# Loading and casting the wide pieces of w_in in parts by contraction block

## Chip, cores, metric

One core of a Trainium2 chip; the three later calls of runs ran on three different chips, and each ratio compares runs of one call. The metric is the device time of one execution in microseconds (us), the median of several. The profile's span is some 2 us shorter than that time.

## The reference

```python
# q, k, v: (8, 8, 576, 64) float32; moe_w_in: (512, 2048); moe_w_out: (2048, 512)
q_s = softmax(q, axis=-1); k_s = softmax(k, axis=2)
kv  = einsum('bhsd,bhse->bhde', k_s, v)
a   = einsum('bhsd,bhde->bhse', q_s, kv)          # attention without a score matrix
x   = a.transpose(0, 2, 1, 3).reshape(4608, 512)
out = (gelu_exact(x @ moe_w_in) @ moe_w_out)      # float32
```

## The kernel before

Nine token blocks of 512 pass through a hidden phase (16 row tiles of x @ w_in with GELU; four matmuls, "dm", make a tile) and an output phase. The attention of later batches is spread into these phases. During the first hidden phase, the weights and the inputs of batches 1 to 3 are still arriving. All loads go through one queue, in program order.

```python
    def h_phase(c, ins, group=1, pre={}):
        ...
        for t0 in [0] + list(range(group, NDF)):
            ...
            for dm in range(NDM):
                ...
                for ps, t in zip(pss, ts):
                    nc.tensor.matmul(
                        ps, wi_bf[:, dm, t * 128:(t + 1) * 128], xT[:, dm, :],
                        start=(dm == 0), stop=(dm == NDM - 1),
                    )
            for ps, t in zip(pss, ts):
                nc.scalar.activation(out=g[:, t, :], in_=ps, func=AF.Gelu)
                for f in ins.get(t, []):
                    f()
    ...
    wi = [load_wi(i) for i in range(5)]
    wo = [load_wo(i) for i in range(3)]
    load_main(1, "q", q, 2)
    load_pair(1, "k", k, 2)
    wo.append(load_wo(3, 2))
    load_pair(1, "v", v, 4)
    load(2)
    nc.vector.memset(zeros, 0.0)
    setup_tiles()
    warm(30)                         # matmuls on zeros while the first inputs arrive
    ... # attention of batch 0
    h_phase(0, {
        0: [lambda: cast_wi(2, wi[2], "v")],
        2: [lambda: cast_wi(3, wi[3], "v")],
        4: [lambda: cast_wi(4, wi[4], "v")],
        ...
    }, group=2, ...)
    ... # output phase 0 with the attention of batch 1, hidden phase 1
    load(3)                          # q, k, v of batch 3
    exp_q(2, parts=2)
    exp_k(2)
    exp_q(3)
    exp_k(3)
    table(AF.Gelu)
    y_phase(1, {
        ...
        (1, 15): [lambda: xbar_step(2)],   # DMA transpose of q of batch 2
        (3, 3): [lambda: x_step(2, 0)],    # its first use by PE
        ...
    })
```

The softmax here doesn't subtract the row's maximum and nothing guards it: scores larger than these inputs give would overflow.

## Time and profile before

| | before |
|---|---|
| time, 3 runs at first | 288.45 us median (288.38 to 288.96) |
| span of the profiled run | 286.4 us |
| PE busy | 277.5 us, 97% |

PE (TensorE) is the bound. The prediction reads the rest of the profile, with its lines.

### The profile page before, as it was taken

The numbers are of one execution on the slowest core, as the hardware profiler recorded it, in microseconds if no ns is written. First come the engines' busy times: TensorE is split into PE (matmuls) and PEld (weight loads), VectorE is DVE, ScalarE is ACT, GpSimd is POOL, SyncE is SP. The second block draws the span as 40 slices with busy tenths as digits, with TensorE's granted clock in tenths as the row PEclk, the third lists the DMA queues.
The fourth block names the chain that finished last, engine by engine and source line by source line (L and its number), as shares of the span: only waits on it lengthen the run. The fifth ranks groups of instructions, "written<-read, shape, count | busy, mean of one in ns | idle before, by whom it ended". The sixth has DMA issues, their size and how long they took to land.

```text
span 286.4 us, 3707 instructions
## 1 busy us (share of the span) xinstructions
PE 277.5 (97%) x1464; PEld 132.4 (46%) x1491; DVE 116.3 (41%) x211; ACT 153.6 (54%) x211; POOL 38.6 (13%) x34
## 2 busy tenths in 40 slices
PE   8969999999999999999999999999999999999995
PEld 3524455445445445444544454445444444444443
DVE  7654387217694553344324522362225112110012
ACT  5766684779465824584368526761664165016500
POOL 5830033002020050005000500040002200000000
PEclk9999999999999999999999999999999999999999
DMA  7999999998519939922994289616701600120033
GB/s 231 374 382 387 371 389 304 319 292 218 146 45 251 298 105 243 263 82 76 224 282 116 76 187 276 163 73 159 136 2 58 157 7 0 64 83 2 0 72 74
DMA packets 58384, 50.04 MB, mean 175 GB/s; under 512 B 26496, under 2 KB 48256, under 8 KB 58368
## 3 DMA queue, kind: packets, MB, share of 16 engines
q1 hardware_dynamic: 58208, 49.68, 61.3%
q8 instruction: 11, 0.18, 0.3%
q10 hardware_dynamic: 160, 0.13, 0.1%
q14 instruction: 5, 0.04, 0.0%
HBM read 36.70 MB, written 9.44 MB: 161 GB/s over the span
## 4 chain that ended last, share of the span: by engine, by line
PE 89%; DMA 6%; ACT 2%; issue 1%; DVE 1%; SPq 0%; ACTq 0%
PE ps L340 42%; PE ps L350 40%; DMA w<-in_moe_w_in_dram 4%; DMA f<-in_k_dram 2%; PE ps L309 2%; PE ps L237 2%; PE ps L372 1%; ACT ek L152 1%; PE ps L241 0%; ACT L152 0%; DVE wi_bf L416 0%; PE ps L183 0%; ACT e L152 0%; SPq L105 0%; PE ps L314 0%
## 5 line engine op out<-in xcount | busy, mean ns | idle before, releaser
L345 ACT ACTIVATE g<-ps 128x512 bf16<-128x512 f32 x144 | 85.8, 597 | 104.7 <-PE ps L340 104.7
L340 PE MATMUL ps<-xT,wi_bf 128*128 128x512 bf16 x560 | 131.0, 379 | 2.6 <-DVE wi_bf L416 1.2
L350 PE MATMUL ps<-wo_bf,g 128*128 128x512 bf16 x549 | 123.2, 379 | 0.6
L340 PEld LDWEIGHTS <-wi_bf 128*128 128x128 bf16 x576 | 55.5, 98 | 66.8 <-DVE wi_bf L416 1.7
L350 PEld LDWEIGHTS <-g 128*128 128x128 bf16 x560 | 54.6, 98 | 64.9
L357 DVE COPY y_sb<-ps 128x512 f32<-128x512 f32 x35 | 23.9, 688 | 75.6 <-PE ps L350 72.6
L229 POOL TENSOR_TENSOR e<-e,recq 128x1024 bf16<-128x1024 bf16 (+1 forms) x10 | 27.6, 2760 | 179.6 <-DVE recq L228 141.5
L322 DVE CAST xT<-ps 128x512 bf16<-128x512 f32 x33 | 22.8, 691 | 36.2 <-PE ps L309 27.6
L227 DVE TENSOR_REDUCE qsum<-e 128x16 f32<-128x1024 bf16 (+1 forms) x13 | 21.1, 1622 | 9.0 <-ACT e L152 8.9
L152 ACT ACTIVATE e<-f 128x1024 bf16<-128x1024 f32 (+1 forms) x11 | 15.8, 1442 | 4.4 <-DMA f<-in_q_dram 4.3
L210 DVE CAST v_aug<-f 128x512 bf16<-128x512 f32 x24 | 10.3, 429 | 9.9 <-DMA f<-in_v_dram 9.3
L309 PE MATMUL ps<-qT,kvbd 128*128 128x512 bf16 x32 | 12.2, 381 | 0.8 <-ACT kvbd L196 0.6
L94 ACT ACT_TABLE_LOAD x9 | 11.5, 1283 | 0.9 <-PEq L616 0.7
L152 ACT ACTIVATE ek<-f 128x2048 bf16<-128x2048 f32 x6 | 11.4, 1894 | 0.0
L436 PE MATMUL ps<-kvbd 128*128 128x512 bf16 x35 | 10.0, 452 | 1.2 <-DVE scr L82 1.2
L168 ACT ACTIVATE ek<-f 64x1152 bf16<-64x1152 f32 x8 | 9.3, 1162 | 1.7 <-DMA f<-in_k_dram 1.6
L237 PEld LDWEIGHTS <-ek 128*128 128x128 bf16 x96 | 6.8, 97 | 3.1 <-ACT ek L152 0.6
L237 PE MATMUL ps<-v_aug,ek 128*128 128x129 bf16 x96 | 8.1, 220 | 0.1
L152 ACT ACT_TABLE_LOAD x6 | 7.7, 1283 | 0.1
L427 DVE CAST wo_bf<-w 128x2048 bf16<-128x2048 f32 (+1 forms) x5 | 5.1, 1014 | 5.3 <-DMA w<-in_moe_w_out_dram 5.1
L259 DVE TENSOR_TENSOR kvbd<-ps,rec 64x128 bf16<-64x128 f32 x24 | 6.9, 289 | 0.6
L436 PEld LDWEIGHTS <-kvbd 128*128 128x128 bf16 x35 | 3.8, 114 | 6.4 <-issue 2.8
(46 smaller groups left out, 83.7 us busy)
## 6 DMA issues: line engine op xcount, KB each, us to landing
out_dram<-y_sb SPq DMA_DIRECT2D x32, 256.0 KB, 2.4
f<-in_q_dram SPq DMA_DIRECT2D x6, 1024.0 KB, 8.0
f<-in_k_dram SPq DMA_DIRECT2D x6, 1024.0 KB, 10.9
f<-in_v_dram SPq DMA_DIRECT2D x6, 1024.0 KB, 9.9
w<-in_moe_w_in_dram SPq DMA_DIRECT2D x3, 1024.0 KB, 12.5
w<-in_moe_w_out_dram SPq DMA_DIRECT2D x3, 1024.0 KB, 12.2
f<-in_k_dram SPq DMA_DIRECT2D x4, 576.0 KB, 8.3
f<-in_v_dram SPq DMA_DIRECT2D x8, 288.0 KB, 8.5
```

Source lines behind the costliest of these rows:

```text
L94: nc.scalar.activation(out=scr[:, 1:2], in_=scr[:, 0:1], func=func)
L152: nc.scalar.activation(out=dst[:, i * n:(i + 1) * n], in_=src[:, i * n:(i + 1) * n], func=AF.Exp)
L227: nc.vector.reduce_sum(out=qsum, in_=eq[:, :, hs, :], axis=AX.X)
L229: eng.tensor_tensor(out=eq[:, :, hs, :], in0=eq[:, :, hs, :], in1=recq.unsqueeze(3).to_broadcast([128, J, w, D]), op=ALU.mult,)
L237: nc.tensor.matmul(ps, st[b]["ek"][:, j, hs, :].rearrange("p h d -> p (h d)"), v_aug[b % 2][:, j, hp, 0:PW], start=(j == 0), stop=False,)
L309: nc.tensor.matmul(ps, kvbd[b][:, hp, :], st[b]["qT"][:, :, hp, :], start=True, stop=True)
L322: nc.vector.tensor_copy(out=st[b]["xT"][:, hp, :], in_=ps)
L340: nc.tensor.matmul(ps, wi_bf[:, dm, t * 128:(t + 1) * 128], xT[:, dm, :], start=(dm == 0), stop=(dm == NDM - 1),)
L345: nc.scalar.activation(out=g[:, t, :], in_=ps, func=AF.Gelu)
L350: nc.tensor.matmul(ps, st[c]["g"][:, t, j * 128:(j + 1) * 128], wo_bf[:, t, :], start=(t == 0), stop=(t == NDF - 1),)
L357: nc.vector.tensor_copy(out=y_sb, in_=ps)
L436: nc.tensor.matmul(ps, zeros[:, 0:128], zeros, start=True, stop=True)
```

## The change

The intent: PE should start on the third piece's first contraction block while the last one is still coming. In the diff, `groups={0: 2}` does what `group=2` did; the moved cast keeps its place in VectorE's order.

```diff
-    def h_phase(c, ins, group=1, pre={}):
+    def h_phase(c, ins, groups={}, pre={}):
...
     wi_cols = [256, 256, 512, 512, 512]
+    wi_parts = [1, 1, 4, 2, 2]
     wi_off = [0, 256, 512, 1024, 1536]
 
     def load_wi(i):
+
         w = wst.tile([128, NDM, 512], FP32, tag="w")
         n = wi_cols[i]
-        nc.sync.dma_start(
-            out=w[:, :, 0:n],
-            in_=moe_w_in[:, wi_off[i]:wi_off[i] + n].rearrange("(c p) f -> p c f", p=128),
-        )
+        src = moe_w_in[:, wi_off[i]:wi_off[i] + n].rearrange("(c p) f -> p c f", p=128)
+        d = NDM // wi_parts[i]
+        for c in range(0, NDM, d):
+            nc.sync.dma_start(out=w[:, c:c + d, 0:n], in_=src[:, c:c + d])
         return w
...
-            nc.vector.tensor_copy(out=o, in_=w[:, :, 0:n])
+            d = NDM // wi_parts[i]
+            for c in range(0, NDM, d):
+                nc.vector.tensor_copy(out=o[:, c:c + d], in_=w[:, c:c + d, 0:n])
...
-        4: [lambda: cast_wi(4, wi[4], "v")],
+        6: [lambda: cast_wi(4, wi[4], "v")],
```

More of the change, by code (lines that the diff above doesn't have):

```diff
@@ L331, in h_phase @@
         xT = st[c]["xT"]
-        for t0 in [0] + list(range(group, NDF)):
-            ts = range(t0, t0 + (group if t0 == 0 else 1))
+        t1 = 0
+        while t1 < NDF:
+            t0, t1 = t1, t1 + groups.get(t1, 1)
+            ts = range(t0, t1)
             pss = [psum_h.tile([128, M], FP32, tag="h", name="ps") for t in ts]
@@ L482 @@
         2: [lambda: cast_wi(3, wi[3], "v")],
-        4: [lambda: cast_wi(4, wi[4], "v")],
+        6: [lambda: cast_wi(4, wi[4], "v")],
         9: [lambda: cast_wo(0, wo[0])],
         12: [lambda: cast_wo(1, wo[1])],
-    }, group=2, pre={
+    }, groups={0: 2}, pre={
         1: [lambda: x_step(0, 2)],
@@ L537 @@
         12: [lambda: cast_v_all(2)],
-    }, group=2, pre={
+    }, groups={0: 2}, pre={
         1: [lambda: x_step(1, 3, "s")],
```

## The prediction

> **What bounds the kernel now.** I read the page first, then the chain of waits, then single stretches of the timeline. The page says that the matrix engine is busy for 277.5 of 286.4 us, at the full clock. So only some 9 us can be won by removing waits. The chain that ended last, by engine:
>
> ```profile
> PE 89%; DMA 6%; ACT 2%; issue 1%; DVE 1%; SPq 0%; ACTq 0%
> ```
>
> The 6% of DMA and the 1% of DVE sit in the first 21 us, so I took the same chain in that window:
>
> ```profile
> 1.79 6.37 DMA f<-in_k_dram
> 8.15 0.02 issue
> 8.17 11.47 DMA w<-in_moe_w_in_dram
> 19.64 0.02 issue
> 19.66 1.24 DVE wi_bf L416
> 20.90 0.05 issue
> 20.95 7.30 PE ps L340 x33
> ```
>
> Columns: start, duration, what. The third piece of w_in (1 MiB, columns 512 to 1023, row tiles 4 to 7 of the first hidden phase) lands at 19.64 us, is cast as a whole by VectorE until 20.90, and only then does PE begin tile 4. What PE lost shows in the waits of PE over the whole run (waiter, releaser, total us, times, longest) and in its timeline:
>
> ```profile
> PE ps L340 <- DVE wi_bf L416: 1.2, 1, 1.2
> PE ps L436 <- DVE scr L82: 1.2, 1, 1.2
> ```
> ```profile
> 16.75 2.97 PE L340 MATMUL ps<-xT,wi_bf 128*128 128x512 bf16 x12
> 20.95 10.53 PE L340 MATMUL ps<-xT,wi_bf 128*128 128x512 bf16 x47 [1.23 <-DVE wi_bf L416]
> 31.32 1.03 PE L350 MATMUL ps<-wo_bf,g 128*128 128x512 bf16 x4
> ```
>
> It happened once, and it is the largest single wait that PE has (the other 1.2 is the start). The 1.23 us counts from a modelled end of a matmul. Counted in issue slots: tiles 4 to 15 are 48 matmuls, (31.32 - 20.95) / 48 = 0.216 us each. The last matmul of tile 3 began at 16.75 + 2.97 - 0.38 = 19.34, so the next could have begun at 19.56. It began at 20.95: 1.39 us lost. That is the most the change can win here. Pieces four and five cost PE nothing: no other wait for L416 is listed.
>
> DMA is the other half of the picture. In every half-microsecond from 6.5 to 30 us it moves 346 to 419 GB/s at full share, so 1 MiB takes about 2.7 us (1.049 MB / 0.386) and no byte can come sooner by reordering the issue alone.
>
> **What the Trainium skill says.** "VectorE: DVE Perf Modes", section "The perf-mode tier table", gives 1227 ns for a float32 copy of 2048 elements; the trace has 1227 for L416. Its section "The TRN2 errata" says a fixed cost is paid per instruction, so small ones pay more. The trace agrees: 1227 ns for 2048 and 694 for 1024 elements make 0.52 ns per element plus 161 ns fixed, so my estimate for 512 is 428 ns. "DMA: Bandwidth & Descriptors", section "Bandwidth", advises batches of 1 MiB or more and shows 64 KB far below peak. The trace does not show that loss in a full queue: v's four 288 KB parts complete at 10.39, 11.14, 11.89 and 12.66 us in the completion records, 0.75 us apart or 393 GB/s. "Runtime: NRT & Kernel Launch", section "Instruction fetch mechanics", says that instructions are refilled by DMA in blocks of 16 KiB. The page's instruction queue has 11 packets; the packet records put one of 16,384 bytes at 17.45 us for 1.11 us. It falls into our piece: its first engine completes at 17.64 and its last at 19.64, a spread of 2.00 where the piece before had 0.74. I expect it there again, so the end of the piece stays late.
>
> **The change part by part.**
>
> 1. Loads. Three issues become eight; bytes, row length (2 KB) and order stay. Piece three comes in four 256 KB parts, each one block of the contraction; pieces four and five in halves. Each extra issue costs SyncE about 0.45 us (v's parts), 5 x 0.45 = 2.3 us. SyncE waits from 12.8 to 15.4 us anyway, and the queue has about 7 us of bytes ahead.
>
> 2. Semaphores. In the built program eight of them serve the loads in turn, so an issue waits for the load eight places before. With smaller loads these eight cover fewer bytes. I went through the list: the last w_in half waits for the second narrow w_in piece (15.66 us), when three wide pieces, some 7 us of transfer, are still queued or moving. The first w_out piece goes from 15.42 to about 17.6, its two followers to about 18.3 and 20.1. By then at least 2.5 MiB are ahead. The queue should not run dry, and landings stay.
>
> 3. Casts. 3 x 1227 = 3681 ns become 4 x 428 + 4 x 694 = 4488 ns: 0.81 us more on VectorE, which sits idle 2.32, 1.33 and 1.47 us before the three casts. Off the path. The cast moved from tile 4 to tile 6 keeps its place in VectorE's order, as the ordered listing of both kernels shows.
>
> 4. The wait. The first three parts land by 18.96 at an even rate (19.64 - 0.68) and are cast by 19.4. The last lands at 19.64 and is cast by 19.66 + 0.43 = 20.09; with 0.05 to signal, 20.14. PE starts tile 4 at 19.56 on part one; part four is wanted at 19.56 + 3 x 0.216 = 20.21. No wait is left: 1.39 us earlier. Tile 8 is then wanted at 23.0; its halves land near 20.9 and at 22.19, cast by 21.6 and 22.9. Tile 12 at 26.5; cast by 25.6.
>
> 5. What takes some back. PE next meets transfers at 40 to 46 us. These lines are of the timeline there (POOL, then PE, then DVE):
>
> ```profile
> 42.58 0.66 POOL L174 CAST v_aug<-f 128x576 bf16<-128x576 f32 x1 [3.36 <-DMA f<-in_v_dram]
> 43.33 0.67 POOL L174 CAST v_aug<-f 128x576 bf16<-128x576 f32 x1
> ```
> ```profile
> 41.68 1.06 PE L274 MATMUL ps<-identity,e 128*128 128x128 bf16 x16
> 42.57 1.89 PE L350 MATMUL ps<-wo_bf,g 128*128 128x512 bf16 x8
> 44.30 0.45 PE L183 MATMUL ps<-v_aug,ek 128*128 128x65 bf16 x9
> ```
> ```profile
> 38.70 1.59 DVE L229 TENSOR_TENSOR e<-e,recq 128x1024 bf16<-128x1024 bf16 x1
> 40.44 0.69 DVE L427 CAST wo_bf<-w 128x1024 bf16<-128x1024 f32 x1
> ```
>
> All of these except PE's are held by transfers (q, w_out, v of batch 1), which do not come sooner. PE 1.39 earlier would transpose at 40.29; its second half, at 40.82, wants the DVE product of 40.29: fits. It would resume the output matmuls at 41.18; the cast ends at 41.13: just fits. It would want v at 42.91; the first POOL cast ends at 43.24, about 43.30 with the signal: 0.39 us of new wait. The following v parts, POOL-cast by 44.00 and so on, are wanted later than that. Sum: 1.39 - 0.39 = 1.00 us.
>
> 6. After 50 us PE waits for no transfer in the waits view; exponentials and normalisations follow PE and ScalarE, so the 1.00 us should last to the end. Prediction: 288.45 - 1.0 = 287.45 us.
>
> **Rivals.** First, the gain is given back at 43 us: if v of batch 1 landed 0.5 us later, or a cast of w_out became last, only 0.5 would remain (288.0). For it speaks that PE would arrive within 0.1 us of three other events; against it that the queue was saturated and stays in order. Second, more and smaller loads starve the queue: the eight semaphores then hold fewer bytes, and each hole delays all that follows. A hole of 1 us would bring back 288.4, one of 2 us 289.4. Against it: v's parts at 393 GB/s, and the count of queued bytes in step 2. Third, the whole 1.39 stays (287.05), if v happened to land sooner; a saturated queue speaks against it. Fourth, the parts do not help because PE waits for the whole region: then nothing changes (288.45). The changed program has separate waits of PE for each block of tile 4, which speaks against it.
>
> **Range and chances.** The steps give 286.9 to 288.0 and three runs before spread over 0.6 us, so I take 286.9 to 288.2. Two per cent is 5.8 us, over four times the removable wait, so faster by that is next to impossible; slower by that would need several holes in the queue. Faster 0.01, same 0.98, slower 0.01.
>
> **What would show it.** Right: PE runs from tile 3 into tile 4 near 19.56 us, with no wait for the wide w_in casts; four casts of about 428 ns, the last starting near 19.66; PE reaches the output phase near 29.9; a new wait of about 0.4 us for the POOL cast of v near 43; afterwards everything 1.0 us earlier. Wrong: DMA share below 1 between 15 and 40 us, the last part after 19.8, v of batch 1 after 42.7, or a new wait of PE behind 50 us.

## The result, and the profile after

The changed kernel took 288.10 us (median of 6 runs, 287.70 to 288.33) against 288.45 (6 runs, 288.06 to 288.96). The ratio is 0.9984, with a 95% interval of 0.9971 to 0.9997. Ratios here are the mean time of one kernel's fast runs over that of the other's fast runs of the same rounds, so not quite the ratio of the medians quoted. The gain is about 0.4 us, not 1.0, though the time lies within the predicted range.

The chain that ended last, by engine, from the page after:

```profile
PE 89%; DMA 5%; DVE 4%; ACT 1%; issue 0%; SPq 0%; DVEq 0%; ACTq 0%
```

The same chain of the changed kernel, its first 50 us (start, duration, what):

```profile
16.19 1.35 DVE xT L322 x2
17.54 0.04 issue
17.58 12.68 PE ps L342 x58
30.26 10.36 PE ps L352 x48
```

The third piece has left the chain. Where the kernel before had a transfer of 11.47 us and a cast, PE now runs through from 17.58 us to the output phase. PE and then VectorE in the timeline of the changed kernel:

```profile
16.93 13.33 PE L342 MATMUL ps<-xT,wi_bf 128*128 128x512 bf16 x60
30.10 10.52 PE L352 MATMUL ps<-wo_bf,g 128*128 128x512 bf16 x48
```
```profile
17.45 1.43 DVE L422 CAST wi_bf<-w 128x512 bf16<-128x512 f32 x4
20.67 0.69 DVE L422 CAST wi_bf<-w 128x1024 bf16<-128x1024 f32 x1 [1.80 <-DMA w<-in_moe_w_in_dram]
```

PE reaches the output phase at 30.10 us instead of 31.32, although this run began its first GELU 0.18 us later: 1.40 us won, as step 4 has it. But the four casts run back to back from 17.45 us. They did not wait for the last part at 19.6. In this run that part had landed by 18.42 (completion records: sixteen for each load, one from each transfer engine), 0.43 us after the first GELU. A whole piece as late as that would have cost PE nothing either (table below). So the 1.40 us of this pair of profiles come from the early landing, and the pair does not show what the parts are worth.

Then the gain was given back, though not where the prediction looked. The first use of the transposed q of batch 2 by PE (timeline, before and then after; in brackets, idle and releaser):

```profile
75.15 0.38 PE L309 MATMUL ps<-qT,kvbd 128*128 128x512 bf16 x1
```
```profile
74.72 0.38 PE L309 MATMUL ps<-qT,kvbd 128*128 128x512 bf16 x1 [0.60 <-DMA qT<-e]
```

The lead shrinks from 1.20 us to 0.43 in this one step and stays at 0.44 to the last phase. This is a new wait of PE behind 50 us, which the prediction lists as a sign of being wrong. The issue of that transpose by SyncE, before and then after, and the chain after:

```profile
70.64 2.08 SPq L293 DMA_TRANSPOSE qT<-e  x1
```
```profile
69.44 3.20 SPq L293 DMA_TRANSPOSE qT<-e  x1
```
```profile
69.44 5.23 DMA qT<-e
74.68 0.04 issue
74.72 0.38 PE ps L309
```

It is issued 1.20 us earlier, as everything that follows PE is, but lands only 0.39 earlier: 5.23 us after its issue instead of 4.43. Ahead of it in the queue are q, k and v of batch 3 and one output store. They had landed by 71.50 us before and by 72.88 after. Those loads do not follow PE: q began to land at 60.01 us in both profiles, v at 68.97 and 68.98. In the run after, one engine's share of v came 1.02 us behind the other fifteen (0.04 before).

### The profile page after: what moved, and what is told of

Read it like the earlier page. It is cut to its first block, busy times and chain, and to the rows that moved or that the text cites. A ratio compares the mean times of both kernels' runs of the same rounds, so it can differ in the third digit from the quotient of the medians.

```text
span 286.2 us, 3744 instructions
## 1 busy us (share of the span) xinstructions
PE 279.2 (98%) x1491; PEld 132.6 (46%) x1491; DVE 116.8 (41%) x216; ACT 153.5 (54%) x211; POOL 38.5 (13%) x34
## 4 chain that ended last, share of the span: by engine, by line
PE 89%; DMA 5%; DVE 4%; ACT 1%; issue 0%; SPq 0%; DVEq 0%; ACTq 0%
PE ps L342 40%; PE ps L352 38%; PE ps L442 3%; DMA f<-in_k_dram 3%; PE ps L309 2%; DMA qT<-e 2%; PE ps L237 2%; PE ps L374 1%; DVE qsum L227 1%; DVE xT L322 1%; DVE kvbd L198 1%; PE ps L183 1%; PE ps L274 0%; ACT L152 0%; DVE e L229 0%
```

## The experiments

Two questions. What made the third piece late in the first profile and not in the second? And what held the transpose?

**Theory A**: a 16 KiB instruction packet occupied one of the sixteen transfer engines for 1.11 us, and whether that delays the third piece is near chance. **Rival B**: the piece is late for its bytes alone. **Theory C**: the transpose waits for the queue ahead of it, which drains when it drains. **Rival D**: the transpose takes longer by itself.

**The kernel before, again.** No edit.

> The kernel before, unchanged, against itself: the noise that every later ratio is read against, and a second look at the landing of w_in's third piece. Theory A (the piece was late because a 16 KiB instruction packet fell on one transfer engine in its last half microsecond, a near miss that can go either way): ratio 1.000 within 0.002, single runs spread by about 0.8 us, and the piece lands either at 19.6 with 1.2 us of PE wait, or near 18.4 with a PE wait under 0.3. Theory B (the piece is late for its bytes alone): it lands at 19.6 again, within 0.3, whatever the packet does.

Measured: 288.68 us (287.49 to 289.17), ratio 1.0002 [0.9983, 1.0022]. Single runs spread over 1.7 us, twice what I expected. Its chain and its largest wait:

```profile
8.59 11.76 DMA w<-in_moe_w_in_dram
20.35 0.02 issue
20.37 1.24 DVE wi_bf L416
21.61 0.05 issue
21.65 2.55 PE ps L340 x11
```
```profile
PE ps L340 <- DVE wi_bf L416: 1.7, 1, 1.7
```

The piece is even later, at 20.35. One engine completes it 3.04 us after the first, where the piece before had 1.5. The A/A run also sets the scale: differences under half a microsecond need profiles, not times.

**The packet later.**

```diff
-    warm(30)
+    warm(24)
```

> The kernel before with 24 warming matmuls in place of 30: 12 PE instructions fewer ahead of the phase, so that PE asks for its next 16 KiB of instructions some 6 matmuls later, near 18.7 us, when the third piece is past. Theory A: the piece lands near 18.4 us, the whole cast ends near 19.7, PE waits 0.1 to 0.3 us instead of 1.2, with no part of the change. PE is then about 1.2 us early at 65 us and gives some of it back at the transposed q of batch 2: 287.6 to 288.2. Theory B: 19.6 and 1.2 us as before, 288.4.

Measured: 288.10 us, ratio 0.9986 [0.9971, 1.0002]. The packet comes at 19.53 us and the piece lands at 18.90, half a microsecond later than theory A said:

```profile
18.90 0.02 issue
18.93 1.24 DVE wi_bf L416
20.16 0.05 issue
20.21 3.84 PE ps L340 x17
```
```profile
PE ps L340 <- DVE wi_bf L416: 0.2, 1, 0.2
```

The wait drops from 1.2 (1.7 in the second profile) to 0.2 us with no part of the change. This supports A against B. As expected, some of the lead is given back at the transpose (0.36 us).

**v of batch 3 behind the transpose**, on the changed kernel:

```diff
-    load(3)
+    load_main(3, "q", q)
+    load_both(3, "k", k)
...
-        (1, 15): [lambda: xbar_step(2)],
+        (1, 15): [lambda: xbar_step(2), lambda: load_both(3, "v", v)],
```

> The changed kernel with the load of v for batch 3 issued after the DMA transpose of batch 2 and not ahead of it. Theory C (PE's gain of 1.2 us up to 70 us is given back because that transpose queues behind loads that drain at the same time as before): the transpose lands 4.4 to 4.5 us after its issue in place of 5.23, PE waits 0.1 us or less for it, and the time is 287.2 to 287.6, about 0.6 below the changed kernel. Rival D (the transpose takes longer for another cause, such as its own issue): still about 5.2 us, still 0.6 us of wait, 288.1.

Measured: 287.93 us, ratio 0.9981 [0.9966, 0.9996]. The time is above the expected 287.2 to 287.6. In the profile the transpose lands 4.51 us after its issue (the queue ahead was empty at 70.02) and costs PE 0.04 us. That is what C says, but it is no sharp test: the transpose was issued at 70.47 us here, so even behind a queue that is empty at 72.88 it would have been held by its own 4.5 us. The time is too noisy to show anything. Run again beside the changed kernel:

> The changed kernel with v of batch 3 loaded behind the transpose, again, now against the changed kernel itself on the same chip. Theory C: 0.3 to 0.7 us below the run of the changed kernel beside it, that is 287.4 to 287.7 where that one has 288.1; the transpose lands 4.4 to 4.5 us after its issue. Rival D (the queue is not what held the transpose): within 0.15 us of the changed kernel.

Measured: 288.20 us, ratio 0.9986 [0.9960, 1.0013], 0.06 below the median of the changed kernel beside it; the expected 0.3 to 0.7 is missed. In this profile the transpose landed 4.44 us after its issue and cost nothing, but the last part of the third piece came late, and PE waited:

```profile
20.89 0.43 DVE L422 CAST wi_bf<-w 128x512 bf16<-128x512 f32 x1 [1.75 <-DMA w<-in_moe_w_in_dram]
```
```profile
21.38 2.33 PE L342 MATMUL ps<-xT,wi_bf 128*128 128x512 bf16 x10 [0.31 <-DVE wi_bf L422]
```

**The changed kernel, again.** No edit.

> The changed kernel again, beside its variants on one chip. If its gain is real: ratio 0.997 to 0.9995, 287.8 to 288.3. In the profile: no PE wait for a wide w_in cast, and the transpose of batch 2 lands about 1.8 us after the queue ahead of it is empty or 4.4 us after its issue, whichever is later (theory C, from the four profiles of the first call).

Measured: 288.26 us (287.41 to 289.28), ratio 0.9994 [0.9964, 1.0024]: no gain that this could show. Its profile is the case that the prediction described. The last part lands late, at 19.35 us (1.69 after the part before), and PE does not notice. VectorE and PE:

```profile
19.37 0.43 DVE L422 CAST wi_bf<-w 128x512 bf16<-128x512 f32 x1 [1.26 <-DMA w<-in_moe_w_in_dram]
```
```profile
18.23 5.56 PE L342 MATMUL ps<-xT,wi_bf 128*128 128x512 bf16 x25
```

**Only the third piece in parts.** Edit: `wi_parts = [1, 1, 4, 1, 1]`.

> The changed kernel with only the third piece in parts (four), pieces four and five whole again: six issues instead of eight. If the split of the third piece is all that removes the wait: no PE wait at tile 4, and at tiles 8 and 12 none either, time as the changed kernel, 287.9 to 288.2. If the halves of the later pieces matter: a PE wait for a cast at tile 8, about 0.3 to 0.7 us, and 288.4.

Measured: 288.03 us, ratio 0.9989 [0.9972, 1.0006]. No wait at tile 4, and a small one at tile 8: PE's step there is 0.34 us instead of 0.216. The packet had hit piece four, which landed at 22.29. So the split of piece three removes the wait, and the halves of piece four are worth 0.13 us when that piece is hit.

**One half of the change alone.** Loads split and casts whole, then loads whole and casts split:

```diff
-            d = NDM // wi_parts[i]
+            d = NDM
             for c in range(0, NDM, d):
                 nc.vector.tensor_copy(...)     # first kernel; in the second, the same edit at the load
```

> The changed kernel's eight loads, but every piece cast whole, as before. Theory E (splitting the load is what spares the third piece the instruction packet, as in the three profiles with split loads so far): all four parts have landed by 18.4 to 19.0 us, the whole cast ends 1.25 us later, PE waits 0.1 to 0.4 us, time about 288.1 to 288.3. Theory F (the cast in parts is what removes the wait): the last part lands near 19.6 and PE waits 1.2 us or more, 288.5.

> The reverse: the three wide pieces loaded whole as before, cast in parts. Theory E: the piece is hit by the packet again and lands near 19.6 us; the first part is cast 0.43 us later, and PE runs at the pace of the casts (0.36 us a part), so the delay of tile 8 against tile 3 is 0.4 to 1.2 us, against 1.4 before; time 288.2 to 288.5. Theory F: no wait of PE at tile 4 of over 0.6 us, time as the changed kernel.

Measured: 288.00 us (0.9982 [0.9958, 1.0007]) and 288.07 us (0.9992 [0.9962, 1.0022]). In neither profile did the packet hit piece three: in the first it was whole by 18.55 us, in the second piece three kept its place behind the one before. PE had no wait at tile 4 in either (0.14 us at tile 8 in the first). So these two runs do not tell the halves apart, and my theory E (the split load is spared) falls with the late parts in the two runs above. The second is the clearest case for C: its queue drained only at 74.55 us, and this is its waits view:

```profile
PE ps L309 <- DMA qT<-e: 1.1, 1, 1.1
```

**The packet earlier**, on both kernels: `warm(4, 16)`, four 16-column matmuls, after `warm(30)`.

> The kernel before with four 16-column matmuls (8 PE instructions, 0.3 us at most) behind the warming ones, so that PE asks for its next 16 KiB of instructions 8 instructions sooner, between 15.6 and 17.2 us, and the packet can hardly miss the third piece. Theory A: the piece lands 1.5 to 2.4 us after the GELU of tile 0 begins, PE waits 1.2 us or more for its cast, and GELU of tile 8 begins 5.6 to 6.2 us after that of tile 3. If the packet is not what makes the piece late: 4.4 to 4.8 us between those two, as with the packet later.

> The changed kernel with the same four small matmuls, so that the packet falls into the third piece here too. The mechanism of the prediction (PE works on the parts while the last is on its way and being cast): the last part is late by as much as in the whole load beside it, but GELU of tile 8 begins 4.3 to 4.8 us after that of tile 3, 1.4 us less than there. If the change helps only by luck of where the packet falls: 5.6 or more.

Measured: 288.18 us (1.0005 [0.9978, 1.0032]) and 288.21 us (0.9999 [0.9976, 1.0021]). The edit did not do what it was for: the packet came at 18.53 and 17.73 us, 0.26 and 0.20 before the first GELU, and not earlier than in the other runs (0.3 to 0.7 before it). So this pair is two more samples. The whole piece was hit and landed at 21.16:

```profile
22.47 1.25 PE L340 MATMUL ps<-xT,wi_bf 128*128 128x512 bf16 x5 [1.78 <-DVE wi_bf L416]
```

The parts were not hit (last at 18.74) and cost nothing. The forced test of the changed kernel is therefore open; the natural hits have to serve.

**v of batch 3 behind the transpose, on the kernel before.** The same edit.

> The kernel before with v of batch 3 loaded behind the transpose. Theory C says that the transpose ends 4.4 us after its issue there already and PE arrives as it lands, so nothing is to be won: GELU of phase 2 begins 29.27 to 29.32 us after that of phase 1, as before, time 288.4, ratio 1.000 within 0.002. If late v is worth something for itself: ratio below 0.998.

Measured: 287.86 us, ratio 0.9987 [0.9965, 1.0008]. The packet missed piece three here too (it lands at 18.86, PE waits 0.2 us), so the low time says nothing for the edit. The transpose lands 4.43 us after its issue, as in the first profile of the kernel before: nothing to be won there, as expected.

**Everything together**: the changed kernel, v of batch 3 late, `warm(24)`.

> The candidate for the best: the changed kernel, v of batch 3 behind the transpose, and 24 warming matmuls. No wait at tile 4 (4.32 us from GELU of tile 3 to that of tile 8), none for the transpose (29.27 to 29.32 us from phase 1 to phase 2): 1.4 us less than a run of the kernel before in which the packet fell into the piece, 0.3 less than one in which it did not; 287.3 to 287.9, ratio 0.996 to 0.998.

Measured: 287.55 us (287.39 to 288.22, six runs), ratio 0.9971 [0.9950, 0.9992], with no wait at either place. This is the best version measured: some 0.85 us by the mean times, but the interval overlaps that of the changed kernel alone.

**All profiles side by side.** "Late" is when piece three is whole, counted from the start of the first GELU. "Tile 4" is the excess of PE's issue step there over 0.216 us. "Near 43" is the time from GELU of tile 8 to the first GELU of phase 1, over 24.98. "Transpose" is the time from there to the first GELU of phase 2, over 29.28. "Left" is explained below the table. All us, from the start times and completion records of the traces.

| profile | first GELU | left | late | tile 4 | near 43 | transpose |
|---|---|---|---|---|---|---|
| before | 17.81 | 0.52 | 1.83 | 1.39 | 0 | 0 |
| before, again | 18.03 | 1.09 | 2.32 | 1.88 | 0 | 0 |
| before, packet earlier (tried) | 18.79 | 1.09 | 2.37 | 1.94 | 0 | 0 |
| before, packet later | 18.07 | -1.90 | 0.83 | 0.39 | 0 | 0.36 |
| before, v late | 18.06 | -0.31 | 0.80 | 0.37 | 0 | 0 |
| changed | 18.00 | 0.46 | 0.43 | 0 | 0.02 | 0.76 |
| changed, again | 17.56 | 0.49 | 1.79 | 0 | 0.39 | 0 |
| changed, packet earlier (tried) | 17.93 | 0.45 | 0.81 | 0 | 0.43 | 0 |
| changed, v late | 19.03 | -0.38 | 0.81 | 0 | 0 | 0.04 |
| changed, v late, again | 18.52 | 1.12 | 2.35 | 0.47 | 0.58 | 0 |
| all together | 18.35 | -1.97 | 0.78 | 0 | 0 | 0.01 |
| only piece three in parts | 18.27 | 0.43 | 0.51 | 0 | 0 | 0 |
| loads split, casts whole | 18.30 | 0.43 | 0.25 | 0 | 0 | 0.12 |
| loads whole, casts split | 19.24 | -1.23 | 0.82 | 0 | 0 | 1.25 |

Read "late" against "tile 4": with the whole piece the wait is its lateness less 0.43 to 0.44, in the five rows of the kernel before. With loads and casts in parts, lateness of 1.79 costs nothing, and 2.35 costs 0.47, that is lateness less 1.88. So the parts gave PE 1.44 us of slack, in the one profile that puts a number to it. The working of step 4 says 1.45: a cast 0.80 shorter (1.23 - 0.43) and three matmuls of 0.216 done ahead.

"Left" tells when the packet hits. Matching the sixteen completions of each load with those of the load before it, by rank, gives the same picture in all fourteen profiles: one engine, and only one, falls 1.5 to 1.7 us behind, once, in a load that is moving while the packet does. "Left" is how long that engine still had to go in piece three when the packet began (negative: its share was done). In the five profiles where piece three is late it was 0.49 us or more; in the nine others it was 0.46 or less, and a load of the next piece took the delay. The matching is good to some 0.05 us, so the border is about half a microsecond.

## Why the prediction was right or wrong

**Step 4, the wait and its size: right, on two profiles.** 1.39 us was the wait in the first profile, and 1.44 is what the parts hid when piece three was very late. In two profiles the packet happened to hit the parts: lateness of 1.79 cost nothing, and 2.35 cost 0.47. Casts of 128x512 took 0.42 to 0.43 us against the 0.428 estimated.

**Its premise: wrong as a constant.** "I expect it there again, so the end of the piece stays late" failed in the very first profile after. Piece three was hit in three of the four profiles of the kernel before in which the packet had its usual time, and in two of seven with split loads (three of five with whole loads, counting the run with casts split; too few to tell whether splitting changes the odds). I read the wait off one profile; when the packet misses, the kernel before loses only 0.37 to 0.39 us, and that is all there is to win. That is the first part of the missing gain. Whether it hits is a race between the packet and one engine's share of the piece (column "left"). Which engine takes the packet, and so how the race stands, changes from run to run for a reason that stays open, and I could not steer the packet to come earlier.

**Steps 1 to 3: right.** The transfers stayed saturated, parts landed 0.67 to 0.68 us apart (262 kB, 388 GB/s), and no wait came from the eight semaphores or the casts. In step 2 only the times of the w_out issues were off (16.49, 17.14 and 18.90 us instead of 17.6, 18.3 and 20.1), at no cost.

**Step 5, 0.39 us given back near 43 us: right in kind and size, not in every run.** It was 0.39, 0.43 and 0.58 in three of the nine profiles with a part of the change, and 0 to 0.02 in the six others; in the first profile of the changed kernel v had landed 0.19 us sooner and PE had started 0.18 us later. The packet is in this step too: in the profile before, fifteen engines had v's first part at 41.39 us and the one that had fallen behind at 42.52.

**Step 6, "the 1.00 us should last to the end": the step that failed.** I looked for waits of PE in the profile before, found none after 50 us, and took that for slack. There was none: the transpose landed at 75.07 us and PE used it at 75.15. In the profiles it landed at the later of 4.3 to 4.5 us after its issue and about 1.8 us after the queue ahead was empty (72.88 to 74.68, 72.93 to 74.75, 74.55 to 76.39). In the six profiles where the queue decided or nearly did, it took 1.77 to 1.84 us from the empty queue, but 4.34 to 5.72 from its issue and 1.31 to 2.04 from the end of its issue on SyncE. The issue moves with PE; the emptying of the queue doesn't. A PE that is 1.2 us early meets the latter. Moving v of batch 3 behind the transpose emptied the queue by 69.4 to 70.6 us and left at most 0.04 us of this wait in all three profiles where it was done on the changed kernel. By itself that is weak, since PE came to the transpose later in two of them (70.47 and 71.01 us); it is the six drain times that tell C from D. In the profile of the changed kernel this was the larger part of the missing gain. Why the queue drained at 71.4 in one run of the changed kernel and at 72.9 in another is open. So is how much of the mean gain each of the two terms took: a run of the changed kernel can lose either near 43 us or at the transpose, and the start alone (first GELU at 17.56 to 19.24 us) varies more than the change wins.

**The number: in part luck.** The measured gain was 0.35 us by the medians, not 1.00, and the range reached to within 0.25 us of no change at all. In the first pair of profiles the lead at 70 us came from a packet that missed the piece, not from the parts, and it was lost at a place that the prediction did not look at. That 288.10 lies inside the range therefore says little for the steps.

The rivals: the first (given back) is what happened, at the transpose rather than only at v. The second (holes in the queue) and the fourth (no use of parts) did not.

## What to carry to other kernels

Splitting a load and its cast along the contraction lets a matmul chain start one part behind the transfer; its worth is slack against a late piece, the cast's saving plus the matmuls done ahead (1.44 us here), and it pays only as far as the piece is late. When a load lands late, look at its completions one by one: fifteen of the sixteen may have been in time. Before counting a gain as kept, look for the next places where the bound engine meets something that does not move with it, and measure how close they are to being a wait: a profile that shows no wait may show one that is hidden by 0.08 us. And take two profiles of the kernel before, when the change is worth less than half a per cent.

## What the Trainium skill lacked or had wrong

- "Runtime: NRT & Kernel Launch", section "Instruction fetch mechanics", calls the cost of crossing a block "mostly hidden", and does not say what the fetch does to other transfers. In these runs a 16,384-byte packet held one transfer engine for 1.05 to 1.13 us early in the kernel, and that engine's data came 1.5 to 1.7 us late (from the ranks of the completions in fourteen profiles) and stayed behind for the loads that followed; the wait of the matmuls grew from 0.4 us to as much as 1.9.
- "DMA: Bandwidth & Descriptors", section "Bandwidth", gives the rule of 1 MiB or more per DMA. In a queue that is never empty, loads of 256 KiB with 2 KB rows completed 0.67 to 0.68 us apart, 388 GB/s, as fast as whole pieces (2.70 us for 1 MiB).
- "DMA: Bandwidth & Descriptors", section "DMA Transpose (X-bar)", has no latency for a transpose behind other loads: here a 128 x 2048 bf16 transpose within the core's memory took 4.4 to 4.5 us from issue to landing when the queue was empty at its issue (four profiles), and landed about 1.8 us after the transfers ahead of it when they were later (six profiles).
- No page that I read gives the run-to-run spread of the start: the first inputs' landing moved the first GELU between 17.56 and 19.24 us in fourteen profiles of kernels nearly alike up to there, and the 45 runs of the kernel before, on several chips, spread over 2.6 us (287.49 to 290.06), eleven on one chip over 2.5 (287.59 to 290.06).
